# Attention weights of five groups computed on VectorE during the first MoE, in a fused attention and MoE kernel

## Chip, cores, metric

One core of one Trainium2 chip. The metric is the device time of one execution in microseconds.

## The reference

```python
# kv (4, 384, 32, 128) is averaged over 4x4 blocks -> 768 keys per batch, k = v = pooled @ w_sr
s = q @ k.T / sqrt(128)                      # q: 4 batches of 12288 queries
a = exp(s - max) / sum                       # -> x = a @ v, 49152 tokens of 128
h = x @ w_in                                 # 128 -> 2048
out = (h * sigmoid(1.702 * h)) @ w_out       # 2048 -> 128, float32
```

## The kernel before

The tokens are 96 groups of 512. The work goes in two rounds of 48 groups: attention one, first MoE, attention two ("round two"), second MoE. Four kinds of work matter:

- **fill**: TensorE makes three chunks of 128x512 (scores or `h`) into one of two halves of six PSUM banks, and ScalarE turns all three at once (1536 columns) by Exp or by the gelu approximation, into the ring `ag`.
- **drain**: TensorE multiplies the chunks in `ag` by `v` (value products, 129 columns: 128 and the sum of weights) or by `w_out` (512 columns). The sums lie in two further banks, 6 and 7, which VectorE empties.
- **turn**: six transposes on TensorE, for the x tiles below number 72 (`LATER`) of each round. Tiles above make a **trip**: stored to DRAM and loaded back transposed by DMA, 20 tiles (`PART`) at a time.
- the keys of batches 2 and 3, which are made during the first MoE: 16 accumulating loads per batch, then in each of two halves a sum on VectorE (`pooled`) and four transposes and four other small matmuls on TensorE.

A program that runs at build time fixes the order of every engine's instructions: it fills two steps ahead of ScalarE, and drains in what time it reckons TensorE to have left.

```python
def fill_attn(chunks, ps):
    for k, (i, jc) in enumerate(chunks):
        rhs = qTs[i // 4][:, 0, (i % 4) * G:(i % 4 + 1) * G]
        nc.tensor.matmul(ps[:, k, :], kTs[i // GB][:, jc * 128:(jc + 1) * 128], rhs, start=True, stop=True)
    nc.scalar.activation(place([("a",) + c for c in chunks]), ps, AF.Exp, scale=scale)

def fill_moe(chunks, ps):                                   # ... three matmuls with w_in
    nc.scalar.activation(place([("m",) + c for c in chunks]), ps, AF.Gelu_apprx_sigmoid)

def drain_moe(g, fc):
    if fc == 0:
        o_of[g] = acc(("o", g))                             # bank 6 or 7
    nc.tensor.matmul(o_of[g], w_out_sb[:, fc, :], weights(("m", g, fc)), start=(fc == 0), stop=(fc == FCH - 1))
    # ... after the last: nc.vector.transpose(o_sb, o_of.pop(g)), four stores

def background_moe(g):
    n, g = divmod(g, 4 * XS)
    m, odd = divmod(g - 3, 2)                               # trips of x
    if 0 <= m < (4 * XS * G // T - LATER) // PART:
        (bring_back if odd else put_away)(n, m)
    g += n * 4 * XS
    for b, lo in ((2, 2), (3, 20)):
        if lo <= g < lo + 8:
            gate()
            add_kv(b, g - lo)                               # two accumulating loads, issued by GpSimd
        if g in (lo + 9, lo + 13):
            use_kv(b, (g - lo - 9) // 4)                    # pooled on VectorE, then transposes on TensorE
```

The softmax here doesn't subtract the row's maximum and nothing guards it: scores larger than these inputs give would overflow.

## Time and profile before

985.83 us, median of 3 runs (984.55 to 986.24).

| us, profiled run | before |
|---|---|
| span | 986.1 |
| TensorE busy | 963.7 |
| ScalarE busy | 956.0 |
| VectorE busy | 207.7 |
| first MoE: first gelu to the next table load | 353.9, of which ScalarE has no work 8.5 |
| attention two, with the table load before and after it | 132.4 |
| second MoE: first to last gelu | 344.6 |

The last three rows are read from ScalarE's work in order of time. The same stretches by engine, in the kernel before (columns: stretch and its length, then busy us and number of instructions of TensorE, weight loads, VectorE, ScalarE, GpSimd, then the granted clock, DMA share, GB/s):

```profile
149.12:503.04 353.92, 347.19 (x1837) 166.88 (x1835) 53.46 (x115) 345.42 (x256) 42.17 (x50) 0.99 0.65 90
503.04:635.47 132.43, 132.43 (x1415) 94.43 (x1413) 49.60 (x133) 132.02 (x98) 3.27 (x12) 1.00 0.42 77
635.47:980.10 344.63, 344.11 (x1665) 156.41 (x1663) 39.84 (x64) 344.63 (x256) 0.00 (x0) 1.00 0.33 57
```

ScalarE is full in all three but for 8.5 us of the first. Whether TensorE is full too, the prediction reads from the starts of its matmuls. The page's chain of waits for this kernel is divided between the two:

```profile
PE 62%; ACT 26%; DMA 5%; issue 4%; DVE 1%; POOL 1%; POOLq 0%; DVEq 0%; ACTq 0%
```

### The profile page before, as it was taken

How to read it: one execution, taken by the hardware profiler on the slowest of the kernel's cores; microseconds unless marked ns; L12 is line 12 of the kernel's file. 1: busy time of each engine (PE TensorE's matmuls, PEld its weight loads, DVE VectorE, ACT ScalarE, POOL GpSimd, SP SyncE). 2: the span in 40 equal slices, each digit the busy share in tenths (PEclk: the TensorE clock that was granted, in tenths of full speed). 3: DMA queues.
4: the chain of work that ended last, by engine and by line, in shares of the span. 5: the costliest groups of instructions: out<-in, count | busy, mean ns of one | idle time of the engine just before them, and what ended most of it. 6: DMA issues, size and time to landing. Idle time of an engine off the chain costs nothing.

```text
span 986.1 us, 15763 instructions
## 1 busy us (share of the span) xinstructions
PE 963.7 (98%) x6431; PEld 513.1 (52%) x6431; DVE 207.7 (21%) x506; ACT 956.0 (97%) x713; POOL 65.4 (7%) x113
## 2 busy tenths in 40 slices
PE   7899999997999999999999999999999999999997
PEld 3567777543444444444447777754444444444443
DVE  4444333201110111101114433320111010101010
ACT  4999999996999999999999999999999999999997
POOL 3100101320002310000000000000000000000000
PEclk9999999998999999999999999999999999999999
DMA  9897764999628972222276432025772222222222
GB/s 181 160 200 147 108 118 85 121 164 178 115 35 121 157 97 43 35 41 43 41 105 113 86 77 59 2 38 110 136 141 40 44 43 33 38 39 34 41 32 43
DMA packets 335688, 84.99 MB, mean 86 GB/s; under 512 B 309568, under 2 KB 333248, under 8 KB 335296
## 3 DMA queue, kind: packets, MB, share of 16 engines
q1 hardware_dynamic: 305456, 51.34, 31.1%
q0 software_dynamic: 29104, 32.51, 22.0%
q8 instruction: 50, 0.82, 0.3%
q10 hardware_dynamic: 1056, 0.13, 0.1%
q14 instruction: 22, 0.18, 0.1%
HBM read 52.49 MB, written 43.52 MB: 97 GB/s over the span
## 4 chain that ended last, share of the span: by engine, by line
PE 62%; ACT 26%; DMA 5%; issue 4%; DVE 1%; POOL 1%; POOLq 0%; DVEq 0%; ACTq 0%
ACT ag L435 24%; PE banks L440 19%; PE banks L433 18%; PE banks L330 12%; PE banks L319 12%; DMA kvs<-in_kv_dram 4%; ACT ag L321 2%; POOL kvs L161 1%; PE banks L356 1%; DMA x<-in_q_dram 1%; DVE qT L224 1%; PE banks L218 0%; PE banks L129 0%; PE banks L265 0%; DVE xt L346 0%
## 5 line engine op out<-in xcount | busy, mean ns | idle before, releaser
L435 ACT ACTIVATE ag<-banks 128x1536 bf16<-128x1536 f32 x512 | 690.1, 1531 | 8.5 <-PE banks L433 8.5
L433 PE MATMUL banks<-x,w_in_sb 128*128 128x512 bf16 x1536 | 415.9, 379 | 0.4 <-ACT ag L435 0.3
L440 PE MATMUL banks<-ag,w_out_sb 128*128 128x512 bf16 x1536 | 411.5, 380 | 0.5 <-ACT ag L435 0.5
L321 ACT ACTIVATE ag<-banks 128x1536 bf16<-128x1536 f32 (+2 forms) x196 | 260.2, 1451 | 11.7 <-PE banks L319 11.3
L440 PEld LDWEIGHTS <-w_out_sb 128*128 128x128 bf16 x1536 | 149.9, 98 | 180.6 <-issue 1.4
L433 PEld LDWEIGHTS <-w_in_sb 128*128 128x128 bf16 x1536 | 148.4, 98 | 180.4 <-issue 24.1
L447 DVE STREAM_TRANSPOSE o_sb<-banks 128x512 f32<-128x512 f32 x96 | 68.8, 716 | 554.2 <-PE banks L440 554.2
L330 PEld LDWEIGHTS <-ag 128*128 128x128 bf16 x2304 | 150.2, 97 | 48.1 <-issue 1.5
L330 PE MATMUL banks<-v,ag 128*128 128x129 bf16 x2304 | 168.7, 220 | 0.7 <-DVE v L153 0.7
L319 PE MATMUL banks<-qT,kT 128*128 128x512 bf16 x576 | 155.8, 378 | 5.7 <-ACT ag L321 4.1
L319 PEld LDWEIGHTS <-kT 128*128 128x128 bf16 x576 | 48.9, 97 | 33.5 <-issue 4.2
L338 DVE RECIPROCAL rec<-banks 128x3 f32<-128x3 f32 x128 | 23.0, 180 | 132.3 <-PE banks L330 132.3
L346 DVE TENSOR_TENSOR x<-banks,rec 128x384 bf16<-128x384 f32 x80 | 44.6, 558 | 2.8
L161 POOL DMA_DIRECT2D kvs<-in_kv_dram x32 | 40.2, 1307 | 36.9 <-DMA kvs<-in_kv_dram 34.0
L380 POOL MEMSET gate_tile<- 1x8 f32 x38 | 4.5, 119 | 458.0 <-DVE gate_tile L379 458.0
L346 DVE TENSOR_TENSOR xt<-banks,rec 128x384 bf16<-128x384 f32 x48 | 26.8, 558 | 1.7
L358 DVE COPY x<-banks 128x768 bf16<-128x768 bf16 x24 | 13.4, 558 | 24.5 <-PE banks L356 24.5
L356 PE MATMUL banks<-ident,xt 128*128 128x128 bf16 x144 | 11.9, 218 | 0.0
L224 DVE COPY qT<-banks 128x512 bf16<-128x512 bf16 x15 | 9.8, 687 | 5.0 <-PE banks L218 4.9
L195 POOL DMA_DIRECT2D q_bf<-in_q_dram x20 | 9.9, 496 | 5.3 <-DMA x<-in_q_dram 1.9
L356 PEld LDWEIGHTS <-xt 128*128 128x128 bf16 x144 | 9.3, 97 | 1.4
L218 PE MATMUL banks<-ident,x 128*128 128x128 bf16 x64 | 6.0, 224 | 2.6 <-DVE qT L224 1.9
(56 smaller groups left out, 87.7 us busy)
## 6 DMA issues: line engine op xcount, KB each, us to landing
out_dram<-o_sb SPq DMA_DIRECT2D x382, 64.0 KB, 2.0
kvs<-in_kv_dram POOLq DMA_DIRECT2D x32, 384.0 KB, 6.4
q_bf<-in_q_dram POOLq DMA_DIRECT2D x20, 512.0 KB, 6.5
x_bf<-x SPq DMA_DIRECT2D x12, 640.0 KB, 4.7
x<-in_kv_dram POOLq DMA_DIRECT2D x12, 512.0 KB, 12.4
x<-in_q_dram POOLq DMA_DIRECT2D x3, 512.0 KB, 20.3
w_in_sb<-in_moe_w_in_dram POOLq DMA_DIRECT2D x1, 512.0 KB, 5.1
w_out_sb<-in_moe_w_out_dram POOLq DMA_DIRECT2D x1, 512.0 KB, 7.6
```

The source lines that it names most:

```text
L161: nc.gpsimd.dma_start(out=kv_sums[b][:, i2], in_=kv_p[b, i, w, :, i2], **({"accum_op": ADD} if n else {}))
L224: nc.vector.tensor_copy(dst, src)
L319: nc.tensor.matmul(ps[:, k, :], kTs[i // GB][:, jc * 128:(jc + 1) * 128], rhs, start=True, stop=True)
L321: nc.scalar.activation(place([("a",) + c for c in chunks]), ps, AF.Exp, scale=scale)
L330: nc.tensor.matmul(av_of[u][:, k * (C + 1):(k + 1) * (C + 1)], weights(("a", i, jc))[:, o:o + T], vs[i // GB][:, jc, 0:C + 1], start=(jc = ...
L338: nc.vector.reciprocal(rec, ps[:, :, C])
L346: nc.vector.tensor_tensor(to, ps[:, :, 0:C], rec.unsqueeze(2).broadcast_to([128, TS, C]), MUL)
L356: nc.tensor.transpose(ps[:, k, :], xt[:, k, :], ident)
L433: nc.tensor.matmul(ps[:, k, :], w_in_sb[:, fc * 128:(fc + 1) * 128], x[:, g % (4 * XS) * G:(g % (4 * XS) + 1) * G], start=True, stop=True)
L435: nc.scalar.activation(place([("m",) + c for c in chunks]), ps, AF.Gelu_apprx_sigmoid)
L440: nc.tensor.matmul(o_of[g], w_out_sb[:, fc, :], weights(("m", g, fc)), start=(fc == 0), stop=(fc == FCH - 1))
L447: nc.vector.transpose(o_sb, o_of.pop(g))
```

## The change

Its intent: ScalarE looks like the bound and VectorE is idle four fifths of the time. So the 30 score chunks of groups 48 to 52 (the first five of round two) get their exp on VectorE while the first MoE runs: `2^n` by arithmetic on the exponent bits, times a polynomial of degree five. Ten of 96 exps of round two vanish from ScalarE. The value products of these groups are drained early too. To make it fit, the ring shrinks from 108 to 102 chunks (three scratch tiles take the room), of which 30 are set aside for the early weights during the first MoE, the trips begin six groups later, the uses of keys move, and the build-time program reckons with VectorE's queue (`on_dve`).

```diff
+    EARLY = 5
-    AG = 108
+    AG = 102
...
+    def early_fill(i, jc):
+        ps = acc()
+        nc.tensor.matmul(ps, kTs[i // GB][:, jc * 128:(jc + 1) * 128], rhs, start=True, stop=True)
+        steps = early_exp(ps, weights(("a", i, jc)))
+        early_step()
...
+    def early_exp(ps, out):                  # a, b: fp32 scratch, e: int32 scratch, 128x512 each
+        nc.vector.tensor_scalar(a, ps, scale / LN2, -126.0, MUL, MAX)
+        yield 3.5
+        nc.vector.tensor_scalar(b, a, 127.0, MAGIC, MIN, ADD)
+        yield 2.2
+        nc.vector.tensor_scalar(e, b, MAGIC - 127.0, 2.0 ** 23, SUB, MUL)
+        yield 2.2
+        nc.vector.scalar_tensor_tensor(b, b, MAGIC, a, SUB, SUB)
+        yield 3.5
+        nc.vector.tensor_scalar_mul(a, b, COEFFS[5])
+        yield 2.2
+        for k in (4, 3, 2, 1):
+            nc.vector.scalar_tensor_tensor(a, a, COEFFS[k], b, ADD, MUL)
+            yield 3.5
+        nc.vector.scalar_tensor_tensor(out, a, COEFFS[0], e.bitcast(F32), ADD, MUL)
+        yield 3.5
...
-        m, odd = divmod(g - 3, 2)
+        m, odd = divmod(g - 9, 2)
-        for b, lo in ((2, 2), (3, 20)):
+        for b, lo in ((2, 2), (3, 24)):
-            if g in (lo + 9, lo + 13):
-                use_kv(b, (g - lo - 9) // 4)
+            if g in (lo + 10, lo + 12):
+                use_kv(b, (g - lo - 10) // 2)
... (use_kv also waits for the reckoned VectorE time; bookkeeping lines, the 30 places set aside and the ordering of early fills and early drains are cut)
```

More of the change, by code (lines that the diff above doesn't have):

```diff
@@ L9 @@
 F32R = mybir.dt.float32r
+I32 = mybir.dt.int32
 BF = mybir.dt.bfloat16
@@ L16 @@
 LE = mybir.AluOpType.is_le
+SUB = mybir.AluOpType.subtract
+MAX = mybir.AluOpType.max
+MIN = mybir.AluOpType.min
 EQ = mybir.AluOpType.is_equal
@@ L189, in make_v @@
         nc.vector.tensor_copy(vs[b][:, a * K:(a + 1) * K, 0:C], ps[:, :h].rearrange("p (k c) -> p k c", k=K))
+        vs[b, a] = True
     qTs = {}
@@ L285 @@
     slot_of = {}
-    head = 8 * JC
+    head, low = 8 * JC, 0
     def place(chunks):
@@ L295, in place @@
         if head + len(chunks) > AG:
-            head = 0
+            head = low
         lo = head
@@ L307, in room_ahead @@
         busy = set(slot_of.values())
-        return next((n for n in range(AG) if (head + n) % AG in busy), AG)
+        return next((n for n in range(AG - low) if (head - low + n) % (AG - low) + low in busy), AG - low)
+    early = range(NG // R, NG // R + EARLY)
     def weights(c):
+        if c[0] == "a" and c[1] in early:
+            return ag[:, (c[1] - early[0]) * JC + c[2], :]
         return ag[:, slot_of[c], :]
@@ L331, in drain_attn @@
                              vs[i // GB][:, jc, 0:C + 1], start=(jc == 0), stop=(jc == JC - 1))
-            if t % 4 == 3:
+            if t % 4 == 3 and i not in early:
                 del slot_of["a", i, jc]
         if k == TS - 1 and a == 1:
-            close(("av", u), now + EVACUATE)
+            close(("av", u), max(now, dve - 1.0) + EVACUATE)
+            on_dve(4.3)
             ps = av_of.pop(u)[:, 0:TS * (C + 1)].rearrange("p (k c) -> p k c", k=TS)
@@ L348, in drain_attn, with early_step @@
                 turns.append((now + TURN, u // 2))
+    LN2 = 0.6931471805599453
+    MAGIC = 1.5 * 2.0 ** 23
+    COEFFS = (1.0000001192092896, -0.6931469440460205, 0.24022120237350464, -0.05550713464617729, 0.009675541892647743, -0.001327647129073739)
+    def early_fill(i, jc):
+        nonlocal steps
+        ps = acc()
+        rhs = qTs[i // 4][:, 0, (i % 4) * G:(i % 4 + 1) * G]
+        nc.tensor.matmul(ps, kTs[i // GB][:, jc * 128:(jc + 1) * 128], rhs, start=True, stop=True)
+        steps = early_exp(ps, weights(("a", i, jc)))
+        early_step()
+    def early_step():
+        nonlocal steps
+        on_dve(next(steps))
+        if steps.gi_frame.f_locals["last"]:
+            steps = None
+            made.add(early_todo.pop(0))
+    def early_exp(ps, out):
+        last = False
+        a = npool.tile([128, 512], F32, name="ea", bufs=1)
+        b = npool.tile([128, 512], F32, name="eb", bufs=1)
+        e = npool.tile([128, 512], I32, name="ee", bufs=1)
+        nc.vector.tensor_scalar(a, ps, scale / LN2, -126.0, MUL, MAX)
[12 more added lines that the diff above has]
+        nc.vector.scalar_tensor_tensor(out, a, COEFFS[0], e.bitcast(F32), ADD, MUL)
+        last = True
+        yield 3.5
+    made = set()
+    steps, early_todo = None, [(i, jc) for i in early for jc in range(JC)]
     def turn(w):
@@ L414, in background_moe @@
         g += n * 4 * XS
-        for b, lo in ((2, 2), (3, 20)):
+        nonlocal head, low
+        if g == 12:
+            low = EARLY * JC
+            head = max(head, low)
+        if g in (40, 46):
+            i = early[0] + 4 * (g // 46)
+            begun.add(("a", i))
+            background(i)
+        for b, lo in ((2, 2), (3, 24)):
             if lo <= g < lo + 8:
@@ L418, in background_moe @@
                 add_kv(b, g - lo)
-            if g in (lo + 9, lo + 13):
-                use_kv(b, (g - lo - 9) // 4)
+            if g in (lo + 10, lo + 12):
+                use_kv(b, (g - lo - 10) // 2)
     def use_kv(b, a):
+        nonlocal extra_at
         sum_kv(b, a)
+        on_dve(3.5)
+        extra_at = max(extra_at, dve + 1.5)
         extras.extend([(transpose_pooled, b, a), (make_k, b, a), (make_v, b, a)])
@@ L443, in drain_moe @@
         if fc == FCH - 1:
-            close(("o", g), now + EVACUATE)
+            close(("o", g), max(now, dve - 1.0) + EVACUATE)
+            on_dve(3.6)
             o_sb = opool.tile([128, 512], F32, name="o_sb")
@@ L458 @@
     chunks += [(i, jc) for jc in range(2, JC) for i in range(8)]
-    chunks += [(i, jc) for i in range(8, NG) for jc in range(JC)]
+    chunks += [(i, jc) for i in range(8, NG) for jc in range(JC) if i not in early]
     seq, todo = [], []
+    todo_early = [("a", t, a) for t in range(NT) for a in range(2) if (t // TS * TS + TS - 1) // 4 in early]
     for n in range(R):
-        part = chunks[n * NA // R:(n + 1) * NA // R]
+        part = [c for c in chunks if c[0] // (NG // R) == n]
         while part:
@@ L466 @@
             part = part[m:]
-        todo += [("a", t, a) for t in range(n * NT // R, (n + 1) * NT // R) for a in range(2)]
+        todo += [("a", t, a) for t in range(n * NT // R, (n + 1) * NT // R) for a in range(2)
+                 if (t // TS * TS + TS - 1) // 4 not in early]
         flat = [(g, fc) for g in range(n * NG // R, (n + 1) * NG // R) for fc in range(FCH)]
@@ L476 @@
             at[(kind,) + c] = p
-    for kind, t, a in [k for k in todo if k[0] == "a"]:
+    for i in early:
+        for jc in range(JC):
+            at["a", i, jc] = at["a", early[-1] + 1, 0] - 1
+    for kind, t, a in [k for k in todo + todo_early if k[0] == "a"]:
         at["at", t, a] = max(at["a", t // 4, jc] for jc in range(a * K, a * K + K))
@@ L521 @@
     COST = {pool_chunk: (2.5, 2.0), key_chunk: (0.7, 2.0), value_chunk: (0.7, 2.0),
-            transpose_q: (1.2, 4.0), key_and_value: (1.0, 3.0),
+            transpose_q: (1.2, 4.0), early_fill: (1.0, 5.5), key_and_value: (1.0, 3.0),
             transpose_pooled: (1.5, 3.0), make_k: (1.0, 3.0), make_v: (1.5, 3.0), turn: (1.5, 3.5)}
@@ L526, with on_dve @@
     now, end, extra_at = 0.0, [], 0.0
-    done = 0
+    source, dve = None, 0.0
+    def on_dve(cost):
+        nonlocal dve
+        dve = max(dve, now + 1.0) + cost
     def fill(p):
@@ L557 @@
                 f, *args = extras[0]
-            if f and max(now, bank) + COST[f][0] > limit + (LATE if f is turn else 4.5) and room >= 4 * K:
+            if steps and dve <= now + 2.0:
+                early_step()
+            if not f and not steps and early_todo and low and min(slot_of.values()) >= low and (2, 1) in vs and dve <= now + 2.0 and now >= bank:
+                f, args = early_fill, early_todo[0]
+            if f and max(now, bank) + COST[f][0] > limit + (LATE if f is turn else 0.0 if f is early_fill else 4.5) and room >= 4 * K:
                 f = None
@@ L562 @@
                 f(*args)
-                free[last_acc] = now + COST[f][1]
-                extra_at = now + PAUSE
+                free[last_acc] = dve + 1.0 if f is early_fill else now + COST[f][1]
+                if f in (transpose_pooled, make_k, make_v):
+                    on_dve(2.5)
+                extra_at = max(now + PAUSE, dve + 1.5 if f in (transpose_pooled, make_k, make_v) else 0.0)
                 if f is turn:
                     turns.pop(0)
+                elif f is early_fill:
+                    pass
                 else:
@@ L569 @@
                 continue
-            if done == len(todo):
+            if not source:
+                if todo_early and all((i, jc) in made for t in range(todo_early[0][1], todo_early[0][1] + TS)
+                                      for i in [t // 4] for jc in range(JC)):
+                    source = todo_early
+                else:
+                    source = todo
+            if not source:
                 break
-            kind, i, c = todo[done]
+            kind, i, c = source[0]
             needs = at[("at" if kind == "a" else kind, i, c)]
             cost = K * SMALL if kind == "a" else 1.0
-            if needs > n or (kind == "a" and i % TS == c == 0 and at["at", i + TS - 1, 1] > n):
+            first_of = c == 0 and (kind == "m" or i % TS == 0)
+            if source is not todo_early and (needs > n or (kind == "a" and first_of and at["at", i + TS - 1, 1] > n)
+                                             or (kind == "a" and i // 4 in early and (i // 4, JC - 1) not in made)):
+                if first_of:
+                    source = None
                 break
-            start = max(now, end[needs] + HANDOVER)
-            if c == 0 and (kind == "m" or i % TS == 0):
+            start = now if source is todo_early else max(now, end[needs] + HANDOVER)
+            if first_of:
                 start = max(start, bank)
             if start + cost > limit and not (room < 2 * K + 1 or (room < 4 * K and start == now)):
+                if first_of:
+                    source = None
                 break
@@ L583 @@
             (drain_attn if kind == "a" else drain_moe)(i, c)
-            done += 1
-    assert done == len(todo) and not turns and not extras
+            source.pop(0)
+            if not todo_early:
+                low = 0
+            if c == (1 if kind == "a" else FCH - 1) and (kind == "m" or i % TS == TS - 1):
+                source = None
+    assert not todo and not todo_early and not turns and not extras and not early_todo
 _INS = ['q', 'kv', 'w_sr', 'moe_w_in', 'moe_w_out']
```

## The prediction

> **What bounds the kernel now.** I read the page first (busy time, then groups), then ScalarE in order of time, then TensorE in order of time in two steady stretches, then the one hole.
>
> ```profile
> PE 963.7 (98%) x6431; PEld 513.1 (52%) x6431; DVE 207.7 (21%) x506; ACT 956.0 (97%) x713; POOL 65.4 (7%) x113
> ...
> L435 ACT ACTIVATE ag<-banks 128x1536 bf16<-128x1536 f32 x512 | 690.1, 1531 | 8.5 <-PE banks L433 8.5
> L433 PE MATMUL banks<-x,w_in_sb 128*128 128x512 bf16 x1536 | 415.9, 379 | 0.4 <-ACT ag L435 0.3
> ...
> L447 DVE STREAM_TRANSPOSE o_sb<-banks 128x512 f32<-128x512 f32 x96 | 68.8, 716 | 554.2 <-PE banks L440 554.2
> ```
>
> TensorE and ScalarE are both at 97 to 98%, VectorE at 21%. A busy TensorE need not be full, so the next two views ask at what pace each really goes. ScalarE in order of time:
>
> ```profile
> 149.12 79.55 ACT L435 ACTIVATE ag<-banks 128x1536 bf16<-128x1536 f32 x59
> 236.15 1.45 ACT L435 ACTIVATE ag<-banks 128x1536 bf16<-128x1536 f32 x1 [7.48 <-PE banks L433]
> 238.60 264.42 ACT L435 ACTIVATE ag<-banks 128x1536 bf16<-128x1536 f32 x196 [1.00 <-PE banks L433]
> 503.04 1.28 ACT L321 ACT_TABLE_LOAD   x1
> ...
> 634.18 1.28 ACT L435 ACT_TABLE_LOAD   x1
> 635.47 344.63 ACT L435 ACTIVATE ag<-banks 128x1536 bf16<-128x1536 f32 x256
> ```
>
> An activation over three chunks costs 264.42 / 196 = 1.349 us and 344.63 / 256 = 1.346 us start to start (the 1531 ns of the group overlap); I take 1.347. The exps of round two run at the same pace, 86.27 us for 64. From 149.1 to the last end at 980.1 ScalarE has no hole but one: 7.48 + 1.00 us near 230. TensorE in a steady stretch of the first MoE, then while it still drains the attention:
>
> ```profile
> 422.39 0.81 PE L433 MATMUL banks<-x,w_in_sb 128*128 128x512 bf16 x3
> 423.04 0.81 PE L440 MATMUL banks<-ag,w_out_sb 128*128 128x512 bf16 x3
> 423.69 0.81 PE L433 MATMUL banks<-x,w_in_sb 128*128 128x512 bf16 x3
> ```
>
> ```profile
> 150.00 0.86 PE L330 MATMUL banks<-v,ag 128*128 128x129 bf16 x12
> 150.70 0.81 PE L433 MATMUL banks<-x,w_in_sb 128*128 128x512 bf16 x3
> 151.34 0.86 PE L330 MATMUL banks<-v,ag 128*128 128x129 bf16 x12
> ```
>
> Three matmuls of 512 columns start every 0.65 us, so 0.216 us each, back to back; twelve of 129 columns take 0.70 us, 0.058 each. One fill with twelve value products costs TensorE 0.65 + 0.70 = 1.35 us, exactly what ScalarE takes. So **both** engines are full. Going through all starts of matmuls, TensorE's gaps above these paces after 147.8 us sum to 9.1 us around the hole and about 8 us elsewhere, 7 of them after 800 us. The hole itself:
>
> ```profile
> 225.21 1.31 POOL L161 DMA_DIRECT2D kvs<-in_kv_dram  x1 [3.49 <-DMA kvs<-in_kv_dram]
> ...
> 232.67 0.69 DVE L167 TENSOR_TENSOR pooled<-kvs 96x512 bf16<-96x512 f32 x1 [9.64 <-DMA kvs<-in_kv_dram]
> ...
> 233.42 0.50 PE L172 MATMUL banks<-ident,pooled 96*128 96x96 bf16 x4 [6.39 <-DVE pooled L167]
> ```
>
> TensorE stands in its own order before the transposes of batch 2's pooled kv, which wait for the last accumulating load, landed at 232.6. Its DMA shared the engines with the trips of x to DRAM and back (DMA share 1.42 from 205 to 226 us, 0.68 from 160 to 185). After the stall the 512-column matmuls start 0.43 us apart for some 5 us.
>
> **What the Trainium skill says.** (1) "TensorE: Matmul & The Clock Gate", section "Wait — 56ns, not 53.3ns?": about 215.7 ns for N=512 warm and 426.7 cold. The trace agrees: 216, and 430 after the hole. (2) "VectorE: DVE Perf Modes", section "The perf-mode tier table": an fp32 one-source operation in SBUF can run at twice the rate, one with two tensors or a PSUM source at 1x. The trace has no large fp32 tensor_scalar; the add of two fp32 tensors of 96x512 took 0.65 us, which fits 1x. (3) "SBUF — State Buffer", section "Who interferes with whom": VectorE's two-port modes lock GpSimd out of descriptor writing. This trace has no large one-source operation within SBUF during these loads; after the change it can.
>
> **The change, part by part.**
>
> *Removed from ScalarE*: groups 48 to 52 have 5 x 6 = 30 chunks, so 10 activations of round two: 10 x 1.347 = 13.5 us. The built order confirms 86 exps in round two instead of 96.
>
> *Added to VectorE*: per chunk one operation from PSUM (0.69 us, as the 128x512 copy from PSUM), three one-source ones in SBUF (my estimate 0.45; the one 128x512 cast in SBUF took 0.49), six with two fp32 tensors (0.65): 0.69 + 1.35 + 3.9 = 5.9 us, times 30 = 178 us. Busy VectorE goes from 208 to about 385 us. The built order puts the first chunk at the 80th fill of the first MoE, the last ten fills into attention two: one per 187 / 29 x 1.347 = 8.7 us. In these VectorE also has 1.3 output transposes of 0.72, so 6.9 of 8.7 us: it fits, with a fifth to spare.
>
> *Moved on TensorE*: nothing is saved. 28 of the 30 score matmuls and 108 value products (18 tiles x 6) move from round two into the first MoE, with two turns. Counting the matmuls of the built order, at 0.216, 0.058 and 0.056 us (transposes), some 2 us of small ones for the keys:
> - First MoE, 256 fills, ScalarE 344.8. Before: 1498 wide and 339 value products, 323.6 + 19.7 + 2 = 345.3. After: 1501 wide, 429 products, 12 transposes, 324.2 + 24.9 + 0.7 + 2 = 351.8.
> - Attention two. Before, 97 fills: 329 wide, 987 products, 72 transposes: 71.1 + 57.2 + 4.0 = 132.3, ScalarE 132.0 with its table. After, 87 fills: 326, 795, 60: 70.4 + 46.1 + 3.4 = 119.9, ScalarE 118.5.
> - Second MoE, 255 fills. Before: 1524 wide and 165 products, 338.8, ScalarE 344.8. After: 1524 and 267, 344.7, ScalarE 344.8.
>
> Before, ScalarE's sum is 821.6, TensorE's 816.4; 821.6 + 8.5 of hole = 830.1, measured 831.0. After, ScalarE's sum is 808.1, but the larger of the two by stage gives 351.8 + 119.9 + 344.8 = 816.5. **So the 13.5 us taken from ScalarE are worth only some 5 to 6, because TensorE takes over as the bound.**
>
> *Moved as to time*: the trips of x begin six groups later, behind four groups' output stores, after most of batch 2's loads; and the key transposes stand seven fills, 9.4 us, later in TensorE's order (about 236 instead of 227). Even a landing as late as 232.6 would now be in time. The hole of 8.5 us should vanish.
>
> *Smaller ring*: 102 slots, of which the first MoE uses 72. It forces drains earlier but takes no TensorE time.
>
> Sum: 831.0 - 816.5 = 14.5 us, the most if TensorE never waits. From this I take 2 us for waits on its two free banks, whose emptying now queues behind a polynomial step of 0.65 us. 985.8 - 12.5 = **973 us**.
>
> **The rivals.**
> - *ScalarE stays the bound*: both gains count in full, 985.8 - 8.5 - 13.5 = 964. It takes slack on TensorE that the starts do not show: only some 8 us outside the hole. I give it 5%.
> - *Only the hole goes*: moved work costs in the first MoE (6.5 us) what it saves later, or waits eat the 6: about 977. Quite possible, and within the range.
> - *VectorE's queue holds the banks*: output transposes come behind polynomial steps, TensorE waits 0.5 us in each of some 30 groups: 15 us, about 986 with the hole gone. For it: VectorE serves in order and only two banks rotate. Against: the program spaces steps by estimates that appear generous (VectorE used 6.9 of 8.7 us). 7%.
> - *The hole stays or a new one opens* for batch 3, whose loads are issued by GpSimd while VectorE runs two-port operations: 981 and up. Against: keys of batch 3 are wanted three groups (20 us) after the last load is issued, which before landed some 9 us after its issue. 8%.
>
> **Range and chances.** TensorE's work alone, with no gap after 147.8 us, puts the floor at 986.1 - 9.1 - 8.3 = 968.7. The low end is 968. The high end takes the gain of the hole with one or two microseconds of new waits: 979. Faster by over 2% means under 966.1, below TensorE's floor: 3%. Slower by over 2% needs 34 us of new waits against my sum: 2%. Within 2%: 95%.
>
> **What would show it.** Right: ScalarE has 186 exps (now 196), some 8 us of small gaps ended by TensorE, mostly in the first MoE after 250 us, and no gap of 7 us; TensorE's matmuls stay at 0.216 back to back; the first MoE takes about 352 us from first to last activation (before 354), attention two about 120 (131), the second MoE about 345; VectorE is busy some 385 us. Wrong: ScalarE without gaps and a span near 964 (TensorE had slack); TensorE's matmuls waiting for VectorE's transposes or first polynomial steps by more than 3 us in sum (banks); polynomial steps of over 0.8 us; a key transpose again waiting for a landing.

## More of the kernel before

The experiments ran in four jobs on four chips; the median of the kernel before was 985.98 to 986.95 us in them, so a difference across jobs is good to about 1 us.

## The result

975.15 us, median of 4 runs (974.9 to 976.53), against 985.19 for the kernel before. Ratios here and below are the mean of one kernel's runs over the mean of the other's of the same rounds, so not quite the ratio of the medians: 0.9903, 95% interval 0.9885 to 0.9921. That is faster clear of noise, and the same by the 2% verdict.

| us, profiled runs | before | predicted | after |
|---|---|---|---|
| span | 986.1 | | 974.7 |
| VectorE busy | 207.7 | 385 | 385.6 |
| first MoE | 353.9 | 351.8 | 353.2 |
| attention two | 132.4 | 119.9 | 119.9 |
| second MoE | 344.6 | 344.7 | 345.3 |

The page of the changed kernel, its busy times and its chain of waits:

```profile
PE 956.3 (98%) x6431; PEld 513.2 (53%) x6431; DVE 385.6 (40%) x806; ACT 945.0 (97%) x703; POOL 65.8 (7%) x113
...
PE 91%; ACT 4%; DMA 3%; DVE 1%; issue 0%; POOL 0%; ACTq 0%; POOLq 0%
...
L397 DVE SCALAR_TENSOR_TENSOR ea<-ea,eb 128x512 f32<-128x512 f32 x120 | 82.3, 686 | 3.4
...
L394 DVE TENSOR_SCALAR ea<-eb 128x512 f32<-128x512 f32 x30 | 13.2, 440 | 0.9
```

The chain of waits has gone from 62% TensorE and 26% ScalarE to 91% and 4%. The busy shares of the two hardly moved, so it is this line that points to the new bound. It is no proof: `b_both` below, which ScalarE bounds, has 75% and 21%. A step over two fp32 tensors took 0.686 us and a one-source step 0.44, as reckoned (0.65, 0.45).

ScalarE in order of time, changed kernel, to be laid beside the same view in the prediction:

```profile
150.28 95.71 ACT L502 ACTIVATE ag<-banks 128x1536 bf16<-128x1536 f32 x71
247.50 119.00 ACT L502 ACTIVATE ag<-banks 128x1536 bf16<-128x1536 f32 x88 [1.51 <-PE banks L500]
...
431.29 48.80 ACT L502 ACTIVATE ag<-banks 128x1536 bf16<-128x1536 f32 x36 [2.46 <-PE banks L500]
480.45 23.01 ACT L502 ACTIVATE ag<-banks 128x1536 bf16<-128x1536 f32 x17 [0.37 <-PE banks L500]
503.48 1.28 ACT L331 ACT_TABLE_LOAD   x1
```

The gap of 7.48 us is gone. In its place are eight small ones in the first MoE, 6.4 us in all, each ended by TensorE. The stretches by engine, changed kernel:

```profile
150.28:503.48 353.20, 351.58 (x1942) 172.32 (x1940) 221.07 (x403) 346.57 (x256) 43.10 (x52) 1.00 0.66 97
503.48:623.39 119.91, 119.91 (x1207) 82.31 (x1206) 56.25 (x134) 119.04 (x88) 2.71 (x10) 1.00 0.36 68
623.39:968.73 345.34, 344.82 (x1767) 163.12 (x1765) 44.00 (x75) 345.33 (x256) 0.00 (x0) 1.00 0.34 59
```

TensorE has about 100 more matmuls in the first MoE (1942 instead of 1837) and 200 fewer in attention two. Going through the starts of its matmuls as in the prediction (each gap is the time to the next start less 0.216, 0.058 or 0.056 us), TensorE's gaps after 147.8 us sum to 4.5 us; before they were 17.4.

### The profile page after: what moved, and what is told of

Its sections match the earlier page's. It is cut to its first block, busy times and chain, and to the rows that moved or that the text cites. A ratio compares the mean times of both kernels' runs of the same rounds, so it can differ in the third digit from the quotient of the medians.

```text
span 974.7 us, 16041 instructions
## 1 busy us (share of the span) xinstructions
PE 956.3 (98%) x6431; PEld 513.2 (53%) x6431; DVE 385.6 (40%) x806; ACT 945.0 (97%) x703; POOL 65.8 (7%) x113
## 4 chain that ended last, share of the span: by engine, by line
PE 91%; ACT 4%; DMA 3%; DVE 1%; issue 0%; POOL 0%; ACTq 0%; POOLq 0%
PE banks L500 33%; PE banks L507 33%; PE banks L340 13%; PE banks L329 11%; ACT ag L502 3%; DMA qT<-q_bf 2%; ACT ag L331 1%; DMA x<-in_q_dram 1%; PE banks L412 1%; PE banks L370 1%; DVE qT L230 1%; PE banks L224 0%; DVE o_sb L515 0%; PE banks L134 0%; DVE v L194 0%
## 5 line engine op out<-in xcount | busy, mean ns | idle before, releaser
L331 ACT ACTIVATE ag<-banks 128x1536 bf16<-128x1536 f32 (+1 forms) x186 | 247.4, 1466 | 13.2 <-PE banks L329 12.4
L329 PE MATMUL banks<-qT,kT 128*128 128x512 bf16 x546 | 147.8, 378 | 6.9 <-ACT ag L331 4.5
L397 DVE SCALAR_TENSOR_TENSOR ea<-ea,eb 128x512 f32<-128x512 f32 x120 | 82.3, 686 | 3.4
L329 PEld LDWEIGHTS <-kT 128*128 128x128 bf16 x546 | 46.7, 97 | 35.8 <-issue 4.0
L386 DVE TENSOR_SCALAR ea<-banks 128x512 f32<-128x512 f32 x30 | 20.8, 692 | 33.1 <-PE banks L370 32.9
L399 DVE SCALAR_TENSOR_TENSOR ag<-ea,ee 128x512 bf16<-128x512 f32 x30 | 20.6, 687 | 1.4
L392 DVE SCALAR_TENSOR_TENSOR eb<-eb,ea 128x512 f32<-128x512 f32 x30 | 20.6, 688 | 0.9
L394 DVE TENSOR_SCALAR ea<-eb 128x512 f32<-128x512 f32 x30 | 13.2, 440 | 0.9
## 6 DMA issues: line engine op xcount, KB each, us to landing
x<-in_kv_dram POOLq DMA_DIRECT2D x12, 512.0 KB, 12.5
```

The costliest lines, as they stand in the source:

```text
L386: nc.vector.tensor_scalar(a, ps, scale / LN2, -126.0, MUL, MAX)
L397: nc.vector.scalar_tensor_tensor(a, a, COEFFS[k], b, ADD, MUL)
```

## The experiments

The theory: two effects, the hole gone (by the shifts in time alone) and ten activations fewer, of which TensorE, now the bound, lets only a few microseconds through. The rivals: ScalarE still the bound; waits on VectorE; the hole not cured by the shifts. All runs were compared with the kernel before on the same chip.

### 1. The hole, part by part

The kernel before with the trips alone later (`b_trips`):

```diff
-        m, odd = divmod(g - 3, 2)
+        m, odd = divmod(g - 9, 2)
```

> The kernel before with one line of the change: the trips of x to DRAM and back begin six groups later. Theory (the hole near 230 us comes of the trips crowding batch 2's loads): the last load lands by about 224 us instead of 232.6, TensorE reaches the key transposes at 226.9 as before, the hole of 8.5 us shrinks to under 1 us, time about 977 us, ratio 0.991. Rival (the loads are slow by themselves, only the later place of the transposes cures it): the hole stays at 5 us or more, time over 981 us.

979.09 us, ratio 0.9942 (0.9914 to 0.997). ScalarE has no gap in the first MoE: 256 activations in one piece of 345.15 us. The wait of `pooled` on the last load, in `b_trips`:

```profile
224.64 0.69 DVE L167 TENSOR_TENSOR pooled<-kvs 96x512 bf16<-96x512 f32 x1 [0.56 <-DMA kvs<-in_kv_dram]
```

It landed at 224.6 us instead of 232.7, before TensorE came to the key transposes (227.9). So the trips did crowd the loads.

The kernel before with the uses alone later (`b_use`):

```diff
-            if g in (lo + 9, lo + 13):
-                use_kv(b, (g - lo - 9) // 4)
+            if g in (lo + 10, lo + 12):
+                use_kv(b, (g - lo - 10) // 2)
```

> The kernel before with the key transposes of both batches asked for at groups 10 and 12 after the first load instead of 9 and 13; the trips as before. The built order moves them from fill 156 to fill 162 of the program, 6 x 1.347 = 8.1 us later, to about 235 us. Theory: the landing stays near 232.6 us and is just in time, so the hole is under 1.5 us and the time about 977 us. Rival (the landing is held up by something that moves along with the place of use): a hole of over 4 us again, time over 981 us.

979.36 us, ratio 0.9946 (0.9911 to 0.998). The landing was even later than before, 235.5 us, and ScalarE lost 1.19 us. Either part alone cures the hole but for that: one brings the load forward, the other the need for it back. Both runs stayed 2 us above the 977 expected.

The kernel before with all shifts in time, batch 3's loads at group 24 included, and no exp on VectorE (`b_both`):

```diff
-        m, odd = divmod(g - 3, 2)
+        m, odd = divmod(g - 9, 2)
-        for b, lo in ((2, 2), (3, 20)):
+        for b, lo in ((2, 2), (3, 24)):
-            if g in (lo + 9, lo + 13):
-                use_kv(b, (g - lo - 9) // 4)
+            if g in (lo + 10, lo + 12):
+                use_kv(b, (g - lo - 10) // 2)
```

> The kernel before with all shifts in time of the change (trips later, use at 10 and 12, batch 3's loads at group 24), no exp on VectorE. Theory: the hole is gone and nothing else changes: 985.2 - 8.5 = 976.7 us, ratio 0.9915; the whole of VectorE's exp is then worth what separates this from the changed kernel's 975.2, so 1 to 4 us, not 13.5. Rival (ScalarE's 13.5 us are all that came, and the shifts bring nothing): about 985 us.

979.39 us, ratio 0.9948 (0.9925 to 0.9971). Its stretches by engine:

```profile
148.45:494.07 345.62, 342.95 (x1802) 165.88 (x1836) 53.49 (x115) 345.28 (x257) 42.29 (x50) 1.00 0.64 95
494.07:626.56 132.49, 131.27 (x1394) 94.57 (x1416) 49.79 (x133) 132.06 (x98) 3.28 (x12) 1.00 0.39 72
626.56:971.15 344.59, 342.16 (x1629) 156.32 (x1660) 39.67 (x64) 344.59 (x256) 0.00 (x0) 1.00 0.34 59
```

The first MoE takes 345.6 us instead of 353.9, the rest is as before (some matmul records are missing from this trace, so its TensorE column is low). In the profile the hole is worth 8.3 us, as predicted; in the timed runs it is 5.1 us (0.0052 of 985; 6.6 by the medians). The likely reason lies in the runs of the kernel before: its 11 runs in this job had spans from 979.1 to 985.9 us, and by and large the lower its granted clock the longer it took (0.998 in the run of 979.1, 0.993 in that of 985.9, though one of 983.6 also had 0.998); `b_both` stayed within 977.2 to 979.3. So the hole seems to differ in depth from run to run, and the profiled one was deep: that run took 987.93 us, 2.1 more than the median of 985.83. The depth itself, and whether it follows the landing of that one load, was not traced in the other runs.

The changed kernel with the trips put back to where they were (`a_trips_back`), TensorE's order identical:

```diff
-        m, odd = divmod(g - 9, 2)
+        m, odd = divmod(g - 3, 2)
```

> The changed kernel with the trips of x back where they were (three groups after the start). TensorE's order is the same, instruction for instruction. Prediction as on record: a landing as late as 232.6 us would still be in time for the key transposes at about 236 us, so no hole and about 975 to 976 us. Rival (the earlier trips are what makes the hole): it comes back, ScalarE idle by over 4 us near 235 us, time over 979 us.

976.68 us, ratio 0.9916 (0.9887 to 0.9946). `pooled` and the key transposes in `a_trips_back`:

```profile
232.06 0.69 DVE L172 TENSOR_TENSOR pooled<-kvs 96x512 bf16<-96x512 f32 x1 [2.60 <-DMA kvs<-in_kv_dram]
...
236.31 0.34 PE L177 MATMUL banks<-ident,pooled 96*128 96x96 bf16 x4
```

The load landed nearly as late as in the kernel before (232.1 us, there 232.7), and TensorE came to it at 236.3 without a wait, both as the prediction had them. On one chip and in one job, the exp on VectorE is worth about the difference between 0.9948 and 0.9916: 3.2 us, not 13.5. (The two runs also differ in when the trips begin. The changed kernel itself, which has them where `b_both` has, took 975.15 us in another job, 4.2 less than `b_both`.) The intervals of the two ratios overlap, but the ranges of their runs do not (975.1 to 978.1 against 978.94 to 981.12).

### 2. Which engine holds back the ten activations

The changed kernel with 2 of 16 output matmuls of every group left out, a wrong result (`a_light`), and `b_both` with the same (`b_both_light`):

```diff
-        nc.tensor.matmul(o_of[g], w_out_sb[:, fc, :], weights(("m", g, fc)), ...)
+        if fc not in (5, 10):
+            nc.tensor.matmul(o_of[g], w_out_sb[:, fc, :], weights(("m", g, fc)), ...)
```

> The changed kernel with 2 of the 16 output matmuls of each group left out (wrong result on purpose): 192 matmuls of 0.216 us, 41 us less for TensorE, ScalarE's work untouched. Theory (TensorE has become the bound and hides most of the 13.5 us): ScalarE becomes the bound again, its gaps in the first MoE close, time about 964 us, ratio to before 0.978. Rival (ScalarE bounds the changed kernel, or waits on VectorE do): about 974 to 975 us, no change.

> The kernel before with all shifts in time but no exp on VectorE, and the same 192 matmuls left out (wrong result on purpose). Theory: this kernel is bound by ScalarE, so lighter TensorE work brings nothing or 1 us: about 976 us; then the difference to the changed kernel lightened the same way is the whole of the ten activations, 13.5 us. Rival (TensorE bounds this one too): several us under the one with all matmuls.

`b_both_light` took 977.21 us, ratio 0.991 (0.9885 to 0.9934): 41 us less work on TensorE bought it about 2. ScalarE bounds that kernel. `a_light` took 971.73 us, ratio 0.9855 (0.9825 to 0.9884). This is 3.4 us faster than the changed kernel, a third of the 11 us that I expected: the expectation failed. ScalarE in order of time, `a_light`:

```profile
245.88 118.34 ACT L502 ACTIVATE ag<-banks 128x1536 bf16<-128x1536 f32 x88 [1.29 <-PE banks L500]
...
427.80 48.57 ACT L502 ACTIVATE ag<-banks 128x1536 bf16<-128x1536 f32 x36 [2.46 <-PE banks L500]
```

The gaps stand where the changed kernel has them and are nearly as long. TensorE meanwhile had idle time: some 3 us in every 50 in this stage, by the starts of its matmuls. The cause is in the built order. Before the fill at 246 us come twelve output matmuls in a row (eleven here, as one is left out), before that at 428 us 36 value products, six transposes and five output matmuls around one fill. TensorE in order of time, `a_light`, at the first of them:

```profile
241.95 0.81 PE L500 MATMUL banks<-x,w_in_sb 128*128 128x512 bf16 x3
242.59 2.54 PE L508 MATMUL banks<-ag,w_out_sb 128*128 128x512 bf16 x11
244.97 0.81 PE L500 MATMUL banks<-x,w_in_sb 128*128 128x512 bf16 x3
```

Such a lump outlasts the two fills that ScalarE has ahead of it, two activations or 2.7 us: the two longest times from one fill to the next in the first MoE are 3.9 and 3.2 us in the changed kernel and 3.9 and 3.0 in `a_light`, but 1.7 at most in `b_both`. The program had put the lumps there because it reckoned with the full work and a full ring. That can be checked without a chip, by letting the program print its reckoning as it builds: in the first MoE of the changed kernel and of `a_light` it places 72 drains past its own limit for the next fill because too few places in the ring are free (nine of the twelve matmuls in the lump above), in the kernel before and in `b_both` none. Lightening the work does not remove the lumps.

So the next run tells the program what it is ordering (`a_light_told`), with VectorE's steps at their measured size, without which the program does not finish an order:

```diff
-        yield 3.5        # and 2.2
+        yield 3.2        # and 2.0
-            cost = K * SMALL if kind == "a" else 1.0
+            cost = K * SMALL if kind == "a" else 0.0 if c in (5, 10) else 1.0
```

> As a_light (192 output matmuls left out, wrong result on purpose), but the program that orders TensorE's work is told: the left-out matmuls cost it nothing, and VectorE's steps are set at what they took (0.69 and 0.44 us). In the built order of the first MoE the lumps (twelve output matmuls in a row, twice eighteen value products) are gone. Theory (TensorE is the bound of the changed kernel, and a_light kept the gaps only because its order was made for the full work): ScalarE has under 1 us of gaps in the first MoE, time 13.5 us under b_both_light's 977.2, about 964 us. Rival (ScalarE loses these microseconds to VectorE's work or to something else beside TensorE): 970 us or more.

966.02 us (965.61 to 968.19), ratio 0.9785 (0.9736 to 0.9833). ScalarE in order of time, `a_light_told`:

```profile
150.38 263.71 ACT L502 ACTIVATE ag<-banks 128x1536 bf16<-128x1536 f32 x196
414.25 80.77 ACT L502 ACTIVATE ag<-banks 128x1536 bf16<-128x1536 f32 x60 [0.16 <-PE banks L500]
495.03 1.28 ACT L331 ACT_TABLE_LOAD   x1
```

0.16 us of gaps in the whole first MoE, with 28 polynomials running beside it. The built order has no drain past the limit there, and no two fills are more than 1.8 us apart. Against `b_both_light` (another job, 977.21) the ten activations are now worth 11.2 us by the medians, 12.3 by the ratios, of the 13.5. With TensorE lighter and its order made for it, the saving comes through nearly whole; with the lighter work in the old order 5.5 us of it do (`a_light` against `b_both_light`, one job), and with the full work 3 to 4. That is the bound: TensorE's work, in the order in which it comes. The smaller steps in the reckoning are not what did it: built into the changed kernel alone, they leave 71 drains past the limit, the nine above among them (this order was not run).

### 3. Does VectorE hold anything up

The changed kernel without eight of the ten steps per chunk (`a_no_poly`). The order of TensorE is identical. The numbers are wrong; the result still passed the check of correctness, so a pass says nothing of the polynomial.

```diff
-        nc.vector.tensor_scalar(b, a, 127.0, MAGIC, MIN, ADD)      # ... and seven more
-        nc.vector.scalar_tensor_tensor(out, a, COEFFS[0], e.bitcast(F32), ADD, MUL)
+        nc.vector.tensor_scalar_add(out, a, COEFFS[0])
```

> The changed kernel with eight of the ten VectorE operations per chunk left out (wrong result on purpose); TensorE's order is the same, instruction for instruction. VectorE loses 30 x 4.6 = 138 us of work. Theory (VectorE hides fully; TensorE is the bound): within 1 us of the changed kernel, at most 2 us faster. Rival (TensorE's banks wait behind polynomial steps): 5 us or more faster, under 970 us.

975.04 us (974.75 to 975.37), ratio 0.9885 (0.9861 to 0.9909): the changed kernel's time (another job) to 0.1 us. VectorE was busy 237.0 us instead of 385.6, and ScalarE's gaps stood where they were and as long as they were (1.51 at 246, 2.47 at 430 us). So eight of the ten steps cost nothing that shows. The step that reads the bank stayed in; the trace of the changed kernel shows no matmul waiting for it.

### 4. The dose

Three groups on VectorE instead of five (`a_early3`):

```diff
-    EARLY = 5
+    EARLY = 3
```

> The changed kernel with three groups from VectorE instead of five: ScalarE keeps 4 of the 10 activations (5.4 us more work), TensorE has the same work in sum. Theory (TensorE's sum decides): ScalarE's sum 813.5 plus 4 us of TensorE's surplus in the first MoE gives about 817.5 against 816.5, so within 2 us of the changed kernel, 974 to 977 us. Rival (each activation taken from ScalarE counts): 5.4 us slower, about 980.5 us.

976.19 us, ratio 0.9898 (0.9873 to 0.9922), 1.0 us slower than the changed kernel by the medians (975.15, another job) and 1.2 slower than `a_no_poly` of the same job. Four activations more on ScalarE, 5.4 us, cost about 1: attention two grew from 119.9 to 124.3 us, and the first MoE shrank from 353.2 to 349.3.

### 5. Less work for TensorE, right result

If TensorE is the bound, taking work from it should pay, and only here. 96 of 144 transposes leave TensorE: x makes the trip by DMA from tile 24 on instead of 72. `a_turns` is the changed kernel so edited, `b_turns` is `b_both` so edited.

```diff
-    LATER, PART = 72, 20
+    LATER, PART = 24, 28
-        m, odd = divmod(g - 9, 2)
+        m, odd = divmod(g - 3, 2) if g < 5 else divmod(max(g, 9) - 7, 2) if g > 8 else (-1, 0)
```

> The changed kernel with 96 fewer transposes on TensorE (16 turns of 6): x is brought back by DMA from tile 24 on instead of 72, in six trips of 28 tiles instead of 20, the first trip early, the others from group 9. Right result. 96 x 0.056 = 5.4 us less for TensorE, of which the counts by stage leave 816.5 - 812.5 = 4 us on the path. Theory (TensorE's sum decides): about 971 us, and the control (the same on b_both) gains under 1 us. Rival (transposes were hidden anyway): 975 us as before.

> Control: the same 96 transposes taken from the kernel before with all shifts in time (b_both), which has no exp on VectorE. Theory (ScalarE bounds it): within 1 us of b_both, 978 to 980 us. Rival: 3 us or more faster.

`b_turns`: 979.27 us (978.74 to 980.2), as `b_both` had 979.39: nothing, as expected. `a_turns`: 974.27 us (974.03 to 975.03), ratio 0.9871 (0.9837 to 0.9905): 0.9 us better than the changed kernel by the medians of two jobs, where I expected 4. The direction agrees with the theory, but 0.9 us across jobs does not settle it. In its trace the first MoE did shrink, from 353.2 to 348.8 us; but attention two, which starts with 39 value products, a turn and twelve more ahead of one fill, grew a ScalarE gap of 3.06 us, and took 122.1 us instead of 119.9.

A last run tried to remove that lump with VectorE's steps reckoned at their measured size, as in `a_light_told` (`a_turns_paced`):

```diff
-        yield 3.5        # and 2.2
+        yield 3.2        # and 2.0
```

> a_turns with VectorE's steps reckoned at 3.2 and 2.0 units instead of 3.5 and 2.2 (what they took in the changed kernel's trace), so that the thirty chunks are done sooner and attention two does not start with a lump: the built order no longer has 39 value products in a row there, which cost a_turns a gap of 3.06 us on ScalarE. Theory (after the sum, the order in which TensorE's work comes decides): no ScalarE gap of over 2 us in attention two, time 1 to 2 us under a_turns, about 972.5 us. Rival (the gap only moves, since TensorE has the same work): 974 us as a_turns.

974.07 us (973.27 to 976.35), ratio 0.9875 (0.9851 to 0.9898). The gap in attention two fell to 1.61 us, but those of the first MoE grew from 2.8 to 4.5 us in sum. The rival was right: no gain beyond `a_turns`. Neither version can be told from the changed kernel by these intervals; both beat the kernel before.

## Why the prediction was right

975.15 us against 973.0, within 968 to 979. Step by step:

- **Both engines full before, so the larger sum of each stage decides: right.** The three stages after were put at 351.8, 119.9 and 344.7 us and took 353.2, 119.9 and 345.3. (The 131 that the prediction gives for attention two before leaves out the second table load; with it, as in the other figures, it was 132.4.) Runs `a_light_told` and `b_both_light` show the bound by taking TensorE's work away: 11 to 12 us of the 13.5 come through instead of 3 to 4.
- **The hole goes: right, by either of the two shifts alone.** The landing at 232 us that "would now be in time" was run (`a_trips_back`) and was. The size was right in the profile (8.3) and too large for the timed runs (5.1), since the hole varies from run to run. This is most of the 2 us by which the forecast was too low: it took a hole measured in a run of 987.93 us from a median of 985.83. By stage the profiles show a saving of 12.5 us (830.98 to 818.45), as forecast.
- **VectorE has room: right.** 178 us added were reckoned, and VectorE's busy time rose by 177.9. That it fits so closely is partly luck: the 300 steps by themselves took 183.1 us, 6.1 a chunk instead of 5.9.
- **2 us of waits for banks behind a polynomial step: right in size by luck, wrong in cause.** TensorE's gaps in the first MoE after 240 us sum to 2.8 us, but the same kernel without eight of the ten steps has the same time. The waits that the trace names are of the six transposes of a turn on VectorE's division of their tile (0.6 us) and of output matmuls on a copy of batch 3's values (0.9), and `a_no_poly` has both at the same length.
- **What the prediction did not see** is how ScalarE loses its time. It spoke of sums; the losses come at lumps in TensorE's order that are longer than two fills. At full work the two agree, because a full ring makes the lumps. The prediction has it that the smaller ring "takes no TensorE time"; but the first lump, at 244 us and worth a gap of 1.51 us, is such a forced one, and it comes before the first early score matmul (256.6 us). In `a_light` they came apart, and the expectation from sums alone failed by 8 us.

What stays open: whether a better order could use the 4.5 us of TensorE's gaps that remain; two attempts gained 1 us or less.

## What to carry to other kernels

When two engines are both full, as here, expect work taken from one to be worth little more than the slack of the other: add up both engines' work by stage from start-to-start times, before and after, and take the larger. A change that carries several small shifts should be split, since here more than half of the gain came from moving a load's competitors and its use apart, at no cost in work. Before trusting a test that makes one engine lighter, look whether the fixed order still holds the waits of the full work.

## What the Trainium skill lacked or had wrong

- "Perfetto Trace Analysis", section "Identifying the Most-Contended Engine", gives MFU (the matmul work done as a share of the peak; not worked out here) and the busy share of weight loads as the measure of TensorE's headroom. The weight loads were busy 52% before and 53% after, while the sum of the matmuls' start-to-start times left 17.4 and 4.5 us of 820 to 830 us free. The share of weight loads did not tell the engine that was full, or that it became the bound; the starts did, and the chain of waits (62% to 91%) pointed to it.
- "VectorE: DVE Perf Modes", section "The perf-mode tier table", has no row for an operation with a scalar and two tensors; another page has a remark on its throughput, and none has a time for it. Here 128x512 in fp32 took 686 ns, a one-source step within SBUF 418 to 440 ns, one from PSUM 692 ns.
- "SBUF — State Buffer", section "Who interferes with whom", warns of two-port VectorE operations blocking GpSimd's descriptors. Such a delay hardly showed here: of the 90 one-source steps within SBUF, 18 ran while batch 3's loads were issued, and six of the 16 issues overlapped one. One of these took 1463 ns instead of 1306, the other five within 25 ns of their time before; over both batches the median was 1315 ns in both kernels.
- No page has it that an order fixed at build time can make an engine wait for its supplier although the supplier has idle time elsewhere: ScalarE waited 2.46 us at one place with TensorE's full work, and again 2.46 us with 41 us less of it and some 3 us of every 50 idle.
